# Reordering the head of a fused windowed-attention and swish-gated MLP kernel: v on another queue, weights in two loads, scores ahead of v products

## The chip, the cores and the metric

The kernel runs on one core of a Trainium2 chip. The metric is device time in microseconds (us). The core has five engines that run their own instruction streams in order: PE (TensorE, matrix products and transposes), ACT (ScalarE, exp, tanh and copies), DVE (VectorE, elementwise work), POOL (GpSimd, masks, casts, and loads that change the type) and SP (SyncE, loads and stores). SP, ACT and POOL ask for transfers; 16 DMA engines carry them out.

## The reference

```python
# q, k, v: (4, 8, 768, 64) float32; n_sink = 4, window = 128
scores = q @ k.T / 8
keep = (col < 4) | ((row - col >= 0) & (row - col < 128))
a = softmax(where(keep, scores, -1e9))
x = (a @ v) -> (3072, 512)                  # tokens x (heads * 64)
h = x @ w_in                                # (3072, 2048)
g = h / (1 + exp(-beta * h))
out = g @ w_out                             # (3072, 512) float32
```

Each query sees the first four keys (the sinks) and a window of 128.

## The kernel before

**Units.** The tokens are cut into 8 tiles T of 384 rows (two per batch). A unit `n` is one tile of one pair of heads; four units make a tile, 32 units in all. Units 0 to 3 are the first tile, 4 to 7 the second. For one unit: q and k are loaded as float32 by SP (`load_qk`, L520, 192 KB each), cast to bfloat16 (`cast`, L606: q of units 0 to 3 on ACT, all else on POOL), transposed by PE (`transpose_in`, L619) and copied out of PSUM by one DVE or ACT copy (L626). `scores` multiplies in two halves of two PSUM banks each (L665; for units 0 to 3 an additive mask is put there first by PE, L654), and ACT takes the exp (L673) into `E`. `attend` multiplies `E` with v (L736; from units 4 on also the sinks, L725), `normalise` divides (L745, L747), and `transpose_out` (L764, L768) puts the result into `xT`. From unit 12 on, DMA transposes take the place of PE's.

**The MLP.** A tile has 16 blocks of hidden columns. A block is four matmuls, one for each pair of heads `c` (`hidden_matmul`, L780), so that it is complete only when all four units of the tile are in `xT`; then tanh on ACT (L788) and the gate on DVE (L801). The second product (`project`, L809) adds up 16 blocks for each 128 rows. Ahead of tile 0's whole blocks, the matmuls with `c` = 0 to 2 of the first two blocks are issued; only `c` = 3 waits for unit 3.

**Loads.** v of tile 0 comes as three loads on POOL's queue that cast to bfloat16 on the way (`load_v`, L528). w_in comes as four loads on POOL's queue, each of four of the 16 blocks (`load_w_in`, L564, rows of 2 KB in memory), w_out as eight (`load_w_out`, L569). The loads of q and k of units 4 to 7 wait on SP for the landing of the first w_in load.

**What sets the order.** The program is first a graph of steps. `Prog.order` places them by a cost model: at each point the step that can start earliest, and of several the one written first. Each engine then gets a fixed list, with semaphore waits, and executes it strictly in that order. Constants of this model (`QUEUE`, `MIX`, the rates and weights of `transfer`) cost nothing at run time, but they move steps. In stretches where the model expects PE to wait ahead of the first hidden blocks, it puts in filler matmuls (L448), which keep PE's clock up and are no work.

The call that opens the head:

```python
    for n in range(4):
        for x in range(2):
            load_qk(n, x)
    load_v(0, 0, [ADD[0][0]])
    ...
    for n in range(3):
        cast(n)
        if n < 2:
            load_v(0, n + 1, [("k16", n)])
    load_w_in(0, 4, 0, 4, [("q_stage", 2, 0)])
```

Of the kernel before, what the change touches and what calls it, by code (L numbers as in the profile page):

```python
# [18 lines left out]
TT = 384  # L19
# [5 lines left out]
HEAD1 = 32  # L25

# [47 lines left out]
class Node:  # L74
# [3 lines left out]
                 "place", "dma", "mode", "work", "hard")  # L78

    def __init__(self, id, eng):  # L80
        self.id, self.eng = id, eng
        self.items = []
        self.busy = self.lag = 0.0
        self.preds = {}
        self.succs = []
        self.open = 0
        self.ready = self.done = 0.0
        self.place = None
        self.dma = None
        self.mode = 128  # L90
        self.work = 0.0
        self.hard = set()


class Prog:
# [12 lines left out]
    QUEUE = {"sp": (1200.0, 1.0), "act": (1200.0, 1.0), "gp": (2100.0, 3.0)}  # L108
    TAIL, MIX, RING = 900.0, 1.07, 8
# [27 lines left out]
    def op(self, eng, fn, r=(), w=(), x=(), dma=None, busy=100.0, lag=None, after=(), mode=None,  # L137
           seq=None):
# [28 lines left out]
        if dma is not None:  # L167
            self.dma_count[dma] = self.dma_count.get(dma, 0) + 16
            node.dma = (dma, self.dma_count[dma])
            node.work = lag  # L170
# [22 lines left out]
    def landings(self, placed):  # L193
# [9 lines left out]
        while True:  # L203
            now, later = [], []
            for q, ns in queue.items():
                if head[q] < len(ns):
                    at = ns[head[q]].place + self.QUEUE[q][0]
                    (now if at <= t else later).append((at, q))
# [5 lines left out]
            whole = sum(self.QUEUE[q][1] for _, q in now)  # L214
            rate = {q: (self.MIX if len(now) > 1 else 1.0) * self.QUEUE[q][1] / whole for _, q in now}
# [12 lines left out]
    def round(self, took, freed):  # L228
# [10 lines left out]
        def best(e):  # L239
            q = left[e]  # L240
            while head[e] < len(q) and q[head[e]].place is not None:
                head[e] += 1
            if head[e] == len(q):
                return None
            last = q[min(head[e] + self.AHEAD[e], len(q) - 1)].id
            c = [n for n in can[e] if n.id <= last]
            if not c:
                return None
            n = min(c, key=lambda n: (max(n.ready, free[e]), n.id))
            at = max(n.ready, free[e])  # L250
            if n.dma is not None and issued[e] >= self.RING and freed:
                at = max(at, freed[e][issued[e] - self.RING] if issued[e] - self.RING < len(freed[e]) else at)
            return at, n
# [100 lines left out]
def bass_streamingllm_window__then__act_swish_beta_kernel(  # L354
# [42 lines left out]
    stage = {t: [sb(f"{t}_stage{z}", (128, 2, 6, D), F32) for z in range(4)] for t in "qk"}  # L397
    land = [sb(f"land{z}", (128, 2, 2, 3, 2, D), BF16) for z in range(4)]
    qk16 = [sb(f"qk16_{z}", (128, 2, 3, 2, D), BF16) for z in range(NQK)]
    v_aug = sb("v_aug", (128, 4, 2, 6, D + 2), BF16)  # L400
    v_sink = sb("v_sink", (128, NPAIR, 2, D1), BF16)
    k_rows = sb("k_rows", (NPAIR, NSINK, 2, D), BF16)
    k_sink = sb("k_sink", (128, NPAIR, 128), BF16)
    qkT = [sb(f"qkT{z}", (128, 2, 2, TT), BF16) for z in range(4)]
    E = [sb(f"E{z}", (128, 2, 768), BF16) for z in range(2)]
    E_sink = [sb(f"E_sink{z}", (128, TT), BF16) for z in range(2)]
# [25 lines left out]
    def transfer(size, rate, busy=470.0):  # L432
        return {"busy": busy, "lag": size / rate}
# [8 lines left out]
    def constants():  # L442
        fill("dve", ones32[:, :], 1.0, ["ones32"])
        op("act", lambda e: e.activation(scratch[:, :], ones32[:, 0:1], AF.Exp, bias=0.0, scale=1.0),
           r=["ones32"], w=["scratch"], busy=1500.0)
        fill("dve", ones[:, :], 1.0, ["ones"])
        fill("dve", zeros[:, :], 0.0, ["zeros"], busy=350.0)
        P.filler = (lambda e: e.matmul(acc[1][:, 0:128], ones[:, :], ones[:, :], start=True, stop=True),  # L448
# [66 lines left out]
    def load_qk(n, x, after=(), queue="sp"):  # L515
# [5 lines left out]
           dma=f"{name}{pb}_{half}", seq="loads " + queue, **transfer(2 * TT * D * 4, 335))  # L521

    def load_v(T, c, after=()):
# [6 lines left out]
           dma=f"vb{kb}", **transfer(H * 128 * D * 4, 256, 900.0))  # L530

    def land_qk(n, x, after=()):

        b, hp, half, pb = place(n)
        for hh in range(2):
# [3 lines left out]
               dma=f"l{pb}{half}{x}{hh}", **transfer(TT * D * 4, 256, 780.0))  # L539

    def land_v(n, after=()):
        b, hp, _, pb = place(n)
        half = place(n)[2]
        for hh in range(2):
# [3 lines left out]
               w=[("v", pb, 3 * half + c, hh) for c in range(3)], after=after, dma=f"lv{pb}{half}{hh}", **transfer(TT * D * 4, 256, 780.0))  # L548
# [13 lines left out]
    def load_w_in(c, cs, m, ms, after=()):  # L562
        here = slice(m * 128, (m + ms) * 128)
        op("gp", lambda e: e.dma_start(w_in16[:, c:c + cs, here], w_in_src[:, c:c + cs, here]), after=after,  # L564
           w=[("w_in", cc, mm) for cc in range(c, c + cs) for mm in range(m, m + ms)],
           dma=f"wi{c}_{m}", **transfer(cs * ms * 128 * 128 * 4, 345, 740.0))

    def load_w_out(m, ms, after=()):
        op("gp", lambda e: e.dma_start(w_out16[:, m:m + ms, :], w_out_src[:, m:m + ms, :]), after=after,  # L569
           w=[("w_out", mm) for mm in range(m, m + ms)],  # L570
           dma=f"wo{m}", **transfer(ms * 128 * NOUT * 4, 345, 740.0))

    def load_sinks(after=()):
        s = k[:, :, 0:NSINK, :].rearrange("b (g h) s d -> (b g) h (s d)", h=2)
        for hh in range(2):
            op("gp", lambda e, hh=hh: e.dma_start(k_rows[:, :, hh, :].rearrange("n s d -> n s d"),
               k[:, :, 0:NSINK, :].rearrange("b (g h) s d -> h (b g) s d", h=2)[hh]),
               w=[("k_rows", hh)], after=after, dma=f"sk{hh}", busy=650.0, lag=300.0)
            rows = slice(HEAD1 * hh, HEAD1 * hh + NSINK)
            sv = v[:, :, 0:NSINK, :].rearrange("b (g h) s d -> s h (b g) d", h=2)[:, hh]  # L580
            op("gp", lambda e, rows=rows, hh=hh, sv=sv: e.dma_start(v_sink[rows, :, hh, 0:D], sv),
               w=[("v_sink", hh)], r=["v_sink"], after=after, dma=f"sv{hh}", busy=650.0, lag=400.0)
# [17 lines left out]
    def cast(n):  # L600
# [3 lines left out]
        for x, name in enumerate("qk"):  # L604
            eng = "act" if n < 4 and x == 0 else "gp"
# [3 lines left out]
               **(act(TT) if eng == "act" else {"busy": 460.0, "lag": 100.0}))  # L609
# [18 lines left out]

    def keys_of(pb, rows, kb):
        return qkT[pb][rows, kb // 3, 1, kb % 3 * 128:kb % 3 * 128 + 128]  # L630
# [4 lines left out]
    def scores_sink(n):  # L635
        pb = place(n)[3]
        op("pe", lambda e: e.matmul(s_ps[:, 0, 0:TT], k_sink[:, n // 8 * 4 + n % 4, :],  # L637
                                    queries_of(pb, slice(0, 128), 3, 3), start=True, stop=True),
           r=["k_sink", ("k_sink", 0), ("k_sink", 1), ("qkT", pb, 1)], w=["s0"], **pe(TT))
        op("act", lambda e: e.activation(E_sink[n % 2][:, :], s_ps[:, 0, 0:TT], AF.Exp, bias=0.0,  # L640
# [3 lines left out]
    def keys_read(pb, half, runs):  # L644
        return [("qkT", pb, x) for x in sorted({half, *(kb // 3 for kb, _, _ in runs)})]

    def scores(n, c, banks, names):

        _, _, half, pb = place(n)
# [22 lines left out]
        src = (s_ps if names[0] == "s0" else h_ps)[:, 0:2, 0:TT]  # L672
        op("act", lambda e: e.activation(both, src, AF.Exp, bias=0.0, scale=SCALE),  # L673
# [37 lines left out]
    def attend(n):  # L711
# [9 lines left out]
        with P.together("pe"):  # L721
            for mm in range(3):
                m, at = 3 * half + mm, mm * 2 * D1
                if half == 1:
# [4 lines left out]
                       r=[("E_sink", z), "v_sink", ("v_sink", 0), ("v_sink", 1)], w=["av"],  # L729
                       **pe(130))  # L730
                for hh in range(2):
                    kbs = range(m + 1) if half == 0 else (m - 1, m)
                    for x, kb in enumerate(kbs):
# [6 lines left out]
                           w=["av"], **pe(65))  # L740

    def normalise(n):
# [3 lines left out]
           x=["av"], w=[("rden", z)], **dve(225.0))  # L746
# [3 lines left out]
           r=[("rden", z)], x=["av"], w=[("o_norm", o)], **dve(475.0))  # L750
# [56 lines left out]
    def project(T, t, m, bank, name, eng="act", cols=slice(0, NOUT), queue="sp"):  # L807
# [4 lines left out]
        if m == NM - 1:  # L812
# [7 lines left out]
            else:  # L820
# [5 lines left out]
               r=[("out_sb", z)], dma=f"o{z}", **transfer(128 * width * 4, 389))  # L826
# [7 lines left out]
    op("act", lambda e: e.dma_start(beta_stage[:, :], moe_beta.rearrange("(m p) -> m p", p=128)),  # L834
       w=["beta_stage"], dma="beta", busy=500.0, lag=100.0)
    for n in range(3):
        cast(n)
        if n < 2:
            load_v(0, n + 1, [("k16", n)])
    load_w_in(0, 4, 0, 4, [("q_stage", 2, 0)])  # L840

    select(ident32[:, :], ones32[:, :], [[1, 32]], ALU.is_equal, 0.0, 0, -1, ["ones32"], ["ident32"])
    transpose_in(0)
    for n in range(4):
        if n < 3:
            transpose_in(n + 1)
        if n == 0:
            cast(3)
            load_w_in(0, 4, 4, 4, [("q_stage", 3, 0)])
            for m in (8, 12):  # L850
                load_w_in(0, 4, m, 4, [("k_stage", 3, 0)])
            for y in range(4, 8):
                for x in range(2):
                    load_qk(y, x, [("w_in", 0, 0)])
            for c in range(3):
                load_v(1, c, [("w_in", 0, 4)])
            fill("gp", k_sink[:, :, :], 0.0, ["k_sink"], busy=1800.0, after=[("k_stage", 3, 0)])
            load_sinks([("k_stage", 3, 0)])
            masks([("k_stage", 3, 0)])
        scores(n, 0, (s_ps[:, 0, :], s_ps[:, 1, :]), ("s0", "s1"))  # L860
        scores(n, 1, (h_ps[:, 0, :], h_ps[:, 1, :]), ("h0", "h1"))
        if n > 0:
            transpose_out(n - 1, acc[0], "acc0", "dve")
        attend(n)
        normalise(n)
    op("pe", lambda e: nc.tensor.transpose(acc[0][:, 0:16], beta_stage[:, :], ident32[0:16, 0:16]),
       r=["beta_stage", "ident32"], w=["acc0"], **pe(64))
    op("dve", lambda e: e.tensor_scalar(beta_half[:, :], acc[0][:, 0:16], 0.5, None, ALU.mult),
       x=["acc0"], w=["beta"], **dve(100.0))
    for i in range(2):  # L870
# [4 lines left out]
    transpose_out(3, acc[0], "acc0", "act")  # L875
# [12 lines left out]
    for s in range(-2, S_END + NM):  # L888
        i = block_of(s) if 0 <= s < S_END else None
        if i is not None:  # L890
            hidden(i, 3 if i < 2 else 0)
        later = []
        for n, step in AGENDA.get(s, ()):
# [8 lines left out]
            if step in ("a", "b") and n < XBAR:  # L902
                c = "ab".index(step)
                if n < 8 and c == 1:
                    scores(n, c, (h_ps[:, 0, :], h_ps[:, 1, :]), ("h0", "h1"))
                else:
                    scores(n, c, (s_ps[:, 0, :], s_ps[:, 1, :]), ("s0", "s1"))
# [10 lines left out]
        if s == 0:  # L918
            for m in range(0, 8, 2):
                load_w_out(m, 2, [("q_stage", 0, 1)])  # L920
        if s == 2:
            for m in range(8, NM, 2):
                load_w_out(m, 2, [("q_stage", 1, 1)])
# [67 lines left out]
```

## Time and profile before

| what | value |
|---|---|
| median of 3 runs | 229.73 us (229.33 to 229.84) |
| profiled execution, its own time | 229.27 us |
| its span, first to last instruction | 227.5 us |
| granted TensorE clock | 1.0 |
| DMA: packets, bytes, mean rate | 96853, 28.53 MB, 125 GB/s |
| HBM read, written | 27.34 MB, 6.29 MB |
| first complete hidden block of tile 0 closes | from 20.48 us |
| first hidden block of tile 1 | 47.11 us |

All durations below are of the profiled execution; it lies 0.46 us under the median of the runs, and its span 1.77 us under its own time. In the profile's lines, PE is a matmul and PEld the load of its weights, L12 is a line of the kernel, "x4" a count of instructions, and `<-` stands between what is written and what is read. The queues are named q0 (POOL's, which can cast), q1 (SP's) and q10 (ACT's).

### The profile page before, as it was taken

To read this page: it belongs to the slowest core of one execution; us is meant where nothing else is said; L and a number is where in the kernel's file an instruction comes from. 1 tells how busy PE (TensorE), PEld (TensorE's weight loads), DVE (VectorE), ACT (ScalarE), POOL (GpSimd) and SP (SyncE) were. 2 spreads that over 40 slices of the span, in tenths; PEclk is the share of its full clock that TensorE was granted. 3 is DMA by queue.
4 is the path that set the end of the run, shared out by engine and by line. 5 is a ranking of instruction groups with operands and counts; after the bars stand their busy time and mean duration, and the time that the engine had idled before them with its cause. 6 is when DMAs were issued, how large, how long until landed. Compare 5 with 4: busy or idle time off the path is not lost.

```text
span 227.5 us, 4449 instructions
## 1 busy us (share of the span) xinstructions
PE 219.9 (97%) x1759; PEld 121.7 (53%) x1759; DVE 132.2 (58%) x261; ACT 141.9 (62%) x223; POOL 128.6 (57%) x190
## 2 busy tenths in 40 slices
PE   7798989999999999999999999999999999999995
PEld 5355555545555555555555555555555555555544
DVE  5455887569977666566555555665656555443300
ACT  3655886477787666657767666656675764545411
POOL 7788996799975969494939679594600000000000
PEclk9999999999999999999999999999999999999999
DMA  6999999999997999999999989899932202111022
GB/s 163 204 193 220 246 192 208 244 208 176 122 98 117 104 131 151 119 125 128 140 102 142 115 122 162 118 101 147 140 41 63 64 19 63 49 46 46 9 86 92
DMA packets 96853, 28.53 MB, mean 125 GB/s; under 512 B 83376, under 2 KB 93888, under 8 KB 96832
## 3 DMA queue, kind: packets, MB, share of 16 engines
q0 software_dynamic: 62352, 11.32, 65.5%
q1 hardware_dynamic: 34304, 16.79, 33.8%
q8 instruction: 14, 0.23, 0.4%
q10 hardware_dynamic: 176, 0.14, 0.2%
q14 instruction: 7, 0.06, 0.1%
HBM read 27.34 MB, written 6.29 MB: 148 GB/s over the span
## 4 chain that ended last, share of the span: by engine, by line
PE 87%; DMA 7%; ACT 2%; POOL 1%; SPq 1%; issue 1%; DVE 0%; ACTq 0%
PE acc L809 34%; PE h_ps L780 33%; DMA v_aug<-in_v_dram 6%; PE s_ps L736 5%; PE s_ps L693 4%; PE acc L780 2%; PE h_ps L809 2%; DMA k_stage<-in_k_dram 2%; PE s_ps L725 1%; PE s_ps L637 1%; PE s_ps L665 1%; SPq L520 1%; PE s_ps L619 1%; POOL land L538 1%; PE h_ps L665 1%; POOL qk L606 1%
## 5 line engine op out<-in xcount | busy, mean ns | idle before, releaser
L788 ACT ACTIVATE th<-h_ps,beta_half 128x384 f32<-128x384 f32 x120 | 69.5, 581 | 55.6 <-PE h_ps L780 55.1
L809 PE MATMUL acc<-w_out,g 128*128 128x512 bf16 x368 | 101.5, 380 | 0.0
L780 PE MATMUL h_ps<-xT,w_in 128*128 128x384 bf16 x480 | 96.8, 326 | 0.0
L801 DVE SCALAR_TENSOR_TENSOR g<-th,h_ps 128x384 bf16<-128x384 f32 x120 | 65.6, 549 | 45.7 <-ACT th L788 45.0
L780 PEld LDWEIGHTS h_ps<-xT,w_in 128*128 128x128 bf16 x480 | 46.4, 98 | 40.4 <-DVE g L801 0.5
L809 PEld LDWEIGHTS acc<-w_out,g 128*128 128x128 bf16 x368 | 32.8, 98 | 28.0 <-issue 4.0
L538 POOL DMA_DIRECT2D land<-in_q_dram x40 | 30.9, 773 | 28.5 <-DVE rden L745 28.5
L547 POOL DMA_DIRECT2D v_aug<-in_v_dram x40 | 30.9, 773 | 0.0
L538 POOL DMA_DIRECT2D land<-in_k_dram x40 | 30.9, 773 | 0.0
L701 ACT ACTIVATE E<-s_ps 128x1536 bf16<-128x1536 f32 x20 | 28.8, 1442 | 0.3 <-PE s_ps L693 0.3
L707 DVE TENSOR_TENSOR E<-E,mask 128x1536 bf16<-128x1536 bf16 x20 | 19.2, 958 | 16.1 <-ACT E L701 16.1
L817 ACT ACTIVATE out_sb<-acc 128x512 f32<-128x512 f32 x23 | 13.7, 598 | 10.2 <-PE acc L809 10.0
L736 PE MATMUL s_ps<-v_aug,E 128*128 128x65 bf16 x384 | 19.4, 193 | 0.6 <-DMA v_aug<-in_v_dram 0.6
L736 PEld LDWEIGHTS s_ps<-v_aug,E 128*128 128x128 bf16 x384 | 17.0, 97 | 4.7 <-issue 1.4
L747 DVE TENSOR_TENSOR o_norm<-s_ps,rden 128x384 bf16<-128x384 f32 x32 | 17.7, 555 | 0.9
L673 ACT ACTIVATE E<-s_ps 128x768 bf16<-128x768 f32 x16 | 13.0, 809 | 2.3 <-PE s_ps L665 1.9
L626 DVE COPY qkT<-s_ps 128x768 bf16<-128x768 bf16 x10 | 9.5, 955 | 5.8 <-PE s_ps L619 5.7
L693 PE MATMUL s_ps<-qkT 64*128 64x256 bf16 (+2 forms) x144 | 10.1, 254 | 0.0
L745 DVE RECIPROCAL rden<-s_ps 128x6 f32<-128x6 f32 x32 | 6.1, 192 | 6.6 <-PE s_ps L736 6.3
L680 DVE TENSOR_TENSOR E<-E,mask 128x768 bf16<-128x768 bf16 x16 | 9.1, 581 | 1.5 <-ACT E L673 1.4
L528 POOL DMA_DIRECT2D v_aug<-in_v_dram x9 | 8.2, 915 | 2.3 <-DMA w_in<-in_moe_w_in_dram 1.7
L619 PE MATMUL s_ps<-ident,qk 128*128 128x128 bf16 x72 | 7.4, 227 | 2.1 <-POOL qk L606 0.7
(65 smaller groups left out, 145.4 us busy)
## 6 DMA issues: line engine op xcount, KB each, us to landing
out_dram<-out_sb SPq DMA_DIRECT2D x23, 256.0 KB, 2.6
q_stage<-in_q_dram SPq DMA_DIRECT2D x12, 192.0 KB, 7.1
k_stage<-in_k_dram SPq DMA_DIRECT2D x12, 192.0 KB, 8.0
w_in<-in_moe_w_in_dram POOLq DMA_DIRECT2D x4, 512.0 KB, 8.6
w_out<-in_moe_w_out_dram POOLq DMA_DIRECT2D x8, 256.0 KB, 8.4
land<-in_q_dram POOLq DMA_DIRECT2D x40, 48.0 KB, 3.5
land<-in_k_dram POOLq DMA_DIRECT2D x40, 48.0 KB, 3.8
v_aug<-in_v_dram POOLq DMA_DIRECT2D x40, 48.0 KB, 3.4
```

Source lines behind the costliest of these rows:

```text
L538: op("gp", lambda e, d=d, s=s: e.dma_start(d, s), w=[("land", pb, half, x, hh)], after=after, dma=f"l{pb}{half}{x}{hh}", **transfer(TT * D ...
L547: op("gp", lambda e, d=d, s=s: e.dma_start(d, s), w=[("v", pb, 3 * half + c, hh) for c in range(3)], after=after, dma=f"lv{pb}{half}{hh}", ...
L693: op("pe", lambda e, at=at, w=w, kb=kb, qb=qb, nq=nq, hh=hh, rows=rows, bank=bank: e.matmul(s_ps[:, 2 * hh + bank, at:at + w], keys_of(pb, ...
L701: op("act", lambda e: e.activation(E[z][:, :, :], src, AF.Exp, bias=0.0, scale=SCALE), x=list(S_NAMES), w=[("E", z, 0), ("E", z, 1)], **ac ...
L707: op("dve", lambda e: e.tensor_tensor(E[z][:, :, :], E[z][:, :, :], m.unsqueeze(1).to_broadcast([128, 2, 768]), ALU.mult), r=[("E", z, 0), ...
L736: last=(x == len(kbs) - 1): e.matmul(av_ps[:, at + hh * D1:at + hh * D1 + D1], E[z][:, hh, col:col + 128], v_aug[:, pb, hh, kb, 0:D1], sta ...
L747: op("dve", lambda e: e.tensor_tensor(o_norm[o][:, :, :, :].rearrange("p m h d -> p (m h) d"), src[:, :, 0:D], rden[z][:, :].unsqueeze(2). ...
L780: op("pe", lambda e: e.matmul(bank, w_in16[:, c, m * 128:(m + 1) * 128], xT[:, c, T * TT:(T + 1) * TT], start=(c == 0), stop=(c == 3)), r= ...
L788: op("act", lambda e: e.activation(th[i % 3][:, :], bank, AF.Tanh, bias=0.0, scale=beta_half[:, m:m + 1]), x=[name], r=["beta"], w=[("th", ...
L801: op("dve", lambda e: e.scalar_tensor_tensor(g[T % 2][:, m, :], th[i % 3][:, :], 1.0, bank, ALU.add, ALU.mult), r=[("th", i % 3)], x=[name ...
L809: op("pe", lambda e: e.matmul(bank[:, 0:width], g[T % 2][:, m, t * 128:(t + 1) * 128], w_out16[:, m, cols], start=(m == 0), stop=(m == NM ...
L817: op("act", lambda e: e.activation(out_sb[z][:, 0:width], bank[:, 0:width], AF.Copy, bias=0.0, scale=0.5), x=[name], w=[("out_sb", z)], ** ...
```

## The change

- v of units 0 to 3 is loaded by six uncast float32 loads of 128 KB on ACT's queue (`load_v32`), into a new tile `v_stage`, and cast to bfloat16 by POOL (`cast_v`), one step for each unit. `beta` is asked for first; ACT's dummy exp, which brings in the function table, now stands behind these loads.
- w_in comes in two loads of eight blocks each, with rows of 4 KB in memory. The first is placed behind the v cast of unit 0, the second behind that of unit 2.
- For units 0 to 3, `transpose_first` takes the place of `transpose_in`: q and k go to two PSUM banks and are copied out by ACT (q) and DVE (k) separately. q of these units is cast by DVE, not ACT.
- In the written order, the scores of unit `n + 1` stand ahead of the v products of unit `n`. The v products of units 0 to 3 go to `acc[1]`; unit 3's scores use the banks of `tr` and `av`. The outputs of units 0 to 3 are transposed after all four.
- Three blocks, not two, have their first three matmuls issued ahead.
- Of w_out, the first piece is asked for ahead of v of units 4 to 7. The sink tiles have 36 rows, not 128.
- The cost model has a weight for each transfer, and other rates.

```diff
+    def load_v32(x, c):
+        src = v[0, 4 * x:4 * x + 4, c * 128:c * 128 + 128, :].rearrange("h p d -> p h d")
+        op("act", lambda e: e.dma_start(v_stage[:, c, 4 * x:4 * x + 4, :], src), w=[("v_stage", x, c)],
+           dma=f"v{x}{c}", seq="loads act", **transfer(4 * 128 * D * 4, 240, 520.0, 0.45))
+    def cast_v(n):
+        op("gp", lambda e: e.tensor_copy(v_aug[:, n, :, 0:3, 0:D].rearrange("p h c d -> p c h d"),
+                                         v_stage[:, :, 2 * n:2 * n + 2, :]),
+           r=[("v_stage", n // 2, c) for c in range(3)],
+           w=[("v", n, kb, hh) for kb in range(3) for hh in range(2)], busy=460.0, lag=100.0)
...
-            eng = "act" if n < 4 and x == 0 else "gp"
+            eng = "dve" if n < 4 and x == 0 else "gp"
...
+    def transpose_first(n):
+        z = n % NQK
+        for which, name in enumerate("qk"):
+            bank, at = ((tr_ps, "tr"), (av_ps, "av"))[which]
...
+            eng = "act" if which == 0 else "dve"
+            op(eng, lambda e, eng=eng, dst=dst, src=src: (e.copy if eng == "act" else e.tensor_copy)(dst, src),
+               x=[at], w=[("qkT", n, 0) if which else ("qT", n)], **(act(TT) if eng == "act" else dve(480.0)))
...
-    load_v(0, 0, [ADD[0][0]])
+    op("act", lambda e: e.dma_start(beta_stage[:, :], moe_beta.rearrange("(m p) -> m p", p=128)),
+       w=["beta_stage"], dma="beta", busy=500.0, lag=100.0)
     for n in range(4):
         for x in range(2):
             load_qk(n, x)
...
+    for c in range(6):
+        load_v32(c // 3, c % 3)
+    op("act", lambda e: e.activation(scratch[:, :], ones32[:, 0:1], AF.Exp, bias=0.0, scale=1.0),
+       r=["ones32"], w=["scratch"], busy=1500.0)
+    cast(0)
+    cast(1)
+    cast_v(0)
+    load_w_in(0, 8, [("v", 0, 0, 0)])
+    cast(2)
+    cast_v(1)
+    load_sinks(1, [("v", 1, 0, 0)])
...
+    transpose_first(1)
+    first_scores(0)
+    cast(3)
+    cast_v(2)
+    load_w_in(8, 8, [("v", 2, 0, 0)])
+    cast_v(3)
+    for n in range(4):
+        if n < 2:
+            transpose_first(n + 2)
+        if n < 3:
+            first_scores(n + 1)
+        if n == 2:
+            for y in range(4, 8):
+                for x in range(2):
+                    load_qk(y, x, [("w_in", 0, 0)])
...
+            load_w_out(0, 2, [("v", 3, 0, 0)])
+            for c in range(3):
+                load_v(1, c, [("v", 3, 0, 0)])
+        attend(n, acc[1], "acc1")
+        normalise(n, acc[1], "acc1")
+    for n in range(4):
+        transpose_out(n, *((av_ps, "av") if n % 2 else (tr_ps, "tr")), "dve" if n < 2 else "act")
-    for i in range(2):
+    for i in range(3):
         with P.together("pe"):
             for c in range(3):
                 hidden_matmul(i, c)
```

In the changed kernel's lists, POOL executes: the casts of k of units 0 and 1, `cast_v` of unit 0, the first w_in load, `cast_v` of unit 1, the cast of k of unit 2, two small loads of sink keys, the cast of k of unit 3, `cast_v` of unit 2, the second w_in load. On PE, the transposes of q of unit 4 stand ahead of hidden block 8, and those of k of unit 4 ahead of block 10; before, both stood behind block 13.

More of the change, by code (lines that the diff above doesn't have):

```diff
@@ L90, in __init__ @@
         self.mode = 128
-        self.work = 0.0
+        self.work, self.weight, self.late = 0.0, 1.0, 0.0
         self.hard = set()
@@ L213, in landings @@
                 continue
-            whole = sum(self.QUEUE[q][1] for _, q in now)
-            rate = {q: (self.MIX if len(now) > 1 else 1.0) * self.QUEUE[q][1] / whole for _, q in now}
+            weight = {q: queue[q][head[q]].weight for _, q in now}
+            mix = self.MIX if len(now) > 1 and max(weight.values()) > self.HEAVY else 1.0
+            rate = {q: mix * w / sum(weight.values()) for q, w in weight.items()}
             step = min(left[queue[q][head[q]].id] / rate[q] for _, q in now)
@@ L248, in best @@
                 return None
[L249 to L253, printed above, removed]
+            out = issued[e] - self.RING
+            room = freed[e][out] if freed and 0 <= out < len(freed[e]) else 0.0
+            at = {n.id: max(n.ready, free[e], room if n.dma is not None else 0.0) for n in c}
+            n = min(c, key=lambda n: (at[n.id], n.id))
+            return at[n.id], n
         while any(n.place is None for n in self.nodes):
@@ L520, in load_qk @@
         op(queue, lambda e: e.dma_start(d, s), w=[(name + "_stage", pb, half)], after=after,
-           dma=f"{name}{pb}_{half}", seq="loads " + queue, **transfer(2 * TT * D * 4, 335))
+           dma=f"{name}{pb}_{half}", seq="loads " + queue, **transfer(2 * TT * D * 4, 290 if n not in (1, 2) or x else 170, 520.0))
+    def load_v32(x, c):
[7 more added lines that the diff above has]
+           w=[("v", n, kb, hh) for kb in range(3) for hh in range(2)], busy=460.0, lag=100.0)
     def load_v(T, c, after=()):
@@ L547, in land_v @@
             op("gp", lambda e, d=d, s=s: e.dma_start(d, s),
-               w=[("v", pb, 3 * half + c, hh) for c in range(3)], after=after, dma=f"lv{pb}{half}{hh}", **transfer(TT * D * 4, 256, 780.0))
+               w=[("v", pb, 3 * half + c, hh) for c in range(3)], after=after, dma=f"lv{pb}{half}{hh}", **transfer(TT * D * 4, 256, 780.0, 0.4))
     def turn(n):
@@ L644, in keys_read, with scores @@
     def keys_read(pb, half, runs):
-        return [("qkT", pb, x) for x in sorted({half, *(kb // 3 for kb, _, _ in runs)})]
-    def scores(n, c, banks, names):
+        return [("qT", pb), *(("qkT", pb, x) for x in sorted({half, *(kb // 3 for kb, _, _ in runs)}))]
+    def scores(n, c, names):
+        src = h_ps if names[0] == "h0" else s_ps[:, 0:2, :] if names[0] == "s0" else s_ps[:, 2:4, :]
+        banks = [src[:, hh, :] for hh in range(2)]
         _, _, half, pb = place(n)
@@ L832, in bass_streamingllm_window__then__act_swish_beta_kernel, with first_scores @@
             load_qk(n, x)
[L833 to L851 removed]
+    for c in range(6):
[9 more added lines that the diff above has]
+    load_sinks(1, [("v", 1, 0, 0)])
+    select(ident32[:, :], ones32[:, :], [[1, 32]], ALU.is_equal, 0.0, 0, -1, ["ones32"], ["ident32"])
+    transpose_first(0)
+    op("pe", lambda e: nc.tensor.transpose(acc[1][:, 0:16], beta_stage[:, :], ident32[0:16, 0:16]),
+       r=["beta_stage", "ident32"], w=["acc1"], **pe(64))
+    op("dve", lambda e: e.tensor_scalar(beta_half[:, :], acc[1][:, 0:16], 0.5, None, ALU.mult),
+       x=["acc1"], w=["beta"], **dve(100.0))
+    def first_scores(n):
+        pairs = [("s0", "s1"), ("h0", "h1")] if n < 3 else [("tr", "av"), ("s0", "s1")]
+        for c in range(2):
+            scores(n, c, pairs[c])
+    transpose_first(1)
[5 more added lines that the diff above has]
+    for n in range(4):
+        if n < 2:
+            transpose_first(n + 2)
+        if n < 3:
+            first_scores(n + 1)
+        if n == 2:
             for y in range(4, 8):
@@ L854, in bass_streamingllm_window__then__act_swish_beta_kernel @@
                     load_qk(y, x, [("w_in", 0, 0)])
+            fill("gp", k_sink[:, :, :], 0.0, ["k_sink"], busy=550.0, after=[("v", 3, 0, 0)])
+            masks([("v", 3, 0, 0)])
+            load_sinks(0, [("v", 3, 0, 0)])
+            load_w_out(0, 2, [("v", 3, 0, 0)])
             for c in range(3):
[L856 to L869, printed above, removed]
-    for i in range(2):
+                load_v(1, c, [("v", 3, 0, 0)])
[4 more added lines that the diff above has]
+    for i in range(3):
         with P.together("pe"):
@@ L918, in bass_streamingllm_window__then__act_swish_beta_kernel @@
         if s == 0:
-            for m in range(0, 8, 2):
-                load_w_out(m, 2, [("q_stage", 0, 1)])
+            for m in range(2, 8, 2):
+                load_w_out(m, 2, [("w_in", 0, 0)])
         if s == 2:
             for m in range(8, NM, 2):
-                load_w_out(m, 2, [("q_stage", 1, 1)])
+                load_w_out(m, 2, [("w_in", 0, 8)])
             for n in range(8, 12):
```

97 lines of the change are left out of this document (52 added, 45 removed).

## The prediction

> **What bounds the kernel now.** I read the page first, then the busy time by stretches, the chain that ended last, and the DMA landings one issue at a time. The page's first part:
>
> ```profile
> PE 219.9 (97%) x1759; PEld 121.7 (53%) x1759; DVE 132.2 (58%) x261; ACT 141.9 (62%) x223; POOL 128.6 (57%) x190
> ```
>
> Share of the span: TensorE (PE) looks full, so the question is where it is not, and where it is busy with filler. By stretches (start:end, length, then busy time of each engine, clock, DMA share, GB/s):
>
> ```profile
> 12.40:20.50 8.10, 7.51 (x98) 4.77 (x99) 4.93 (x13) 3.61 (x5) 6.38 (x8) 1.00 1.20 200
> 20.50:31.10 10.60, 10.60 (x75) 6.30 (x75) 8.40 (x16) 9.03 (x18) 10.21 (x26) 1.00 1.49 226
> 31.10:33.30 2.20, 1.54 (x19) 0.69 (x18) 1.49 (x3) 2.20 (x5) 2.20 (x4) 1.00 1.24 205
> 33.30:47.00 13.70, 13.45 (x141) 7.09 (x142) 8.84 (x21) 8.33 (x13) 10.04 (x15) 1.00 1.30 227
> 47.00:214.00 167.00, 166.91 (x1290) 91.08 (x1288) 102.10 (x195) 109.64 (x171) 90.36 (x119) 1.00 0.99 105
> ```
>
> From 47 to 214 PE is idle 0.09 us, and the change removes no real PE work, so this kernel can only win or lose ahead of 47 us: in the head, and in the 0.66 us hole at 31 to 33. The chain (start, length, what) in the head:
>
> ```profile
> 6.96 5.41 DMA v_aug<-in_v_dram
> ...
> 12.41 0.30 PE s_ps L736 x4
> ...
> 18.66 0.59 PE acc L780 x3
> 19.25 0.49 PE h_ps L780 x3
> ...
> 19.95 0.49 ACT xT L768
> ...
> 20.48 0.34 PE acc L780
> ...
> 24.28 1.30 PE acc L780 x8
> ```
>
> PE waits for the last v (landing 12.4), works the attention of units 0 to 3, and runs whole hidden blocks (4 matmuls, 0.65 us) from 20.48, with 1.08 us of them done before. Block 8 starts at 24.28+0.65 = 24.93. Landings (last column: us from issue; the issues stand at 8.26, 10.17 and 14.90), and the packets that flowed from 15.0 to 18.5 and from 19 to 22:
>
> ```profile
> w_in<-in_moe_w_in_dram POOLq DMA_DIRECT2D x1, 512.0 KB, 6.6
> ...
> w_in<-in_moe_w_in_dram POOLq DMA_DIRECT2D x1, 512.0 KB, 7.5
> ...
> q_stage<-in_q_dram SPq DMA_DIRECT2D x1, 192.0 KB, 6.6
> ...
> q0 software_dynamic: 693, 0.69, 122.1%
> ...
> q0 software_dynamic: 391, 0.39, 77.6%
> q1 hardware_dynamic: 397, 0.29, 39.7%
> ```
>
> The first w_in piece lands at 14.85, the second at 17.7. q of unit 4, issued by SP at 14.90 behind that first landing, moves no packet until 18.5, while POOL's queue streams weights; then the queues alternate packet for packet. It lands at 21.5. PE needs it only at 28.95, so this delay is hidden now.
>
> **The change, part by part.** All sums are on the profiled execution: span 227.5, time 229.27 (1.77 around it). The median of runs is 229.73, 0.46 above; I shift by that at the end. 0.2% (0.46 us) is about what a measurement of this kernel can tell.
>
> *v on ACT's queue.* Six 128 KB loads asked from 1.3 us on, instead of three cast loads asked at 2.91, 4.98, 6.96 and landed at 10.2, 11.5, 12.4. The first half of v is 1536 rows of 256 bytes, as many packets as the first six q and k loads have (256 rows of 768 bytes each); if the two queues alternate packet for packet, they end together, and the sixth load, k of unit 2, landed at 3.69+5.2 = 8.9. Bounds: 6.1 (the fourth load's landing, if small rows pass faster) to 10.85 (halfway between the landings 10.2 and 11.5, no gain from the queue). I take 8.8, by the row of 8.9 and a little under it, since nothing else is asked for ahead of v on its queue but beta. ACT's issues cost 0.44+6x0.47 = 3.3 us, so its table load (1.28) and dummy exp (0.20), done at 2.77 now, end at about 5.7. An SP issue was once held 1.82 us; three such would free ACT at 9.9. ACT's work for units 0 to 3 is 8 exps at 0.71 to 0.81 and 4 half copies at 0.48, 8.0 us, so 13.8 to 17.9. Neither is last, see below.
>
> *Casts.* DVE casts q0 to q3: not in the trace; between the 0.35 of DVE's 128x384 copy (L768) and POOL's 0.50; off the path, as q lands before k. POOL now waits for v behind k1's cast; queued behind it are w_in, k2 and k3. v lands 8.8, cast 0.50, gap 0.3 (as 6.67 to 6.96): **w_in is issued at 9.6, not 8.26.** Then POOL: issue 0.75, v cast 0.50, k2 0.50, two k_rows issues 1.05, k3 0.50, gaps: k3 is ready at 13.1 instead of 11.43.
>
> *Two w_in DMAs of 1024 KB.* First bytes after 2.1 (the 8 KB beta load's landing), then 5.4: the two pieces before took 5.3 from the last v (12.4) to 17.7, and 2x2.85 = 5.7 by their spacing. I give the 4 KB rows no speed, because no row shows them. First half: 9.6+2.1+5.4 = **17.1**, for blocks 0 to 7. The second is queued right behind, lands about 22.7 and is not last.
>
> *Unit 3's chain.* From k3 13.1: transposes 0.35, copy 0.5, scores 0.6, two exps 1.5, v products 0.55, reciprocal and multiply 0.8, transposes 0.35, copy 0.5, semaphores 0.5: 18.75. Nine opening matmuls of blocks 0 to 2 (1.47) run meanwhile from 17.1, so PE closes block 0 at 18.8, and with 0.49+5x0.65 and the sink transposes (0.18) is ready for block 8 at 22.7.
>
> *What is late next.* In the changed order PE's transposes of q of unit 4 stand ahead of block 8. SP still asks for it when the first w_in DMA lands: 17.1+6.6 = 23.7, cast and semaphores 0.6, transposes 0.17: **block 8 at 24.5.** PE stands 1.6 us. So the gain of the head hangs on w_in plus 7.4, not on attention, which has that much slack. From there 8 blocks 5.2 and the rest of units 4 and 5 (0.50): 30.2, where before was at 31.1. **0.9 gained.**
>
> *The hole at 31 to 33.* Before, products with w_out can't fill it: the first piece, issued 26.41, landed 6.7 later at 33.1. Now that piece is asked for ahead of v of units 4 to 7, and four products (0.86) stand in the hole. I take back 0.66. Bounds: 1.0 if the products also shorten what follows; 0 if k of unit 7 is late. It landed at 29.6, 14.7 after the batch was opened at 14.90; opened at 17.1 it lands by 31.8, or near 30.8 if it shares less with the first weights, and with a 0.55 cast PE wants it landed by 31.1. v of units 4 to 7 (30.4 at the latest now) moves behind one w_out piece, some 1.3 us by the pieces' spacing, and is wanted about 33.8 (34.74 less the 0.9 gained): covered.
>
> *Later.* The same bytes flow, and PE does the same work. The smaller memsets (k_sink was 1.83 on POOL, off the path) and 36-row sinks save nothing on PE. Reordered steps from 47 on cost nothing while v (53.2) and q and k of units 8 to 11 keep ahead; the change puts unit 8's v products six blocks later, which covers them.
>
> Sum: 0.9+0.66 = 1.6. 229.27-1.6 = 227.7 profiled, **228.1** on the runs.
>
> **A rule against it.** POOL's cast at 43.77 took 0.85 instead of 0.50 beside DVE's two-input mask multiply. The Trainium skill (SBUF — State Buffer, on the shared port pair and the "DVE blocks DMA" trap) says that DVE's fp32 SBUF copies also lock GpSimd out, its descriptor writing included; before has no such copy on DVE, so no run yet shows it for casts.
>
> **Rivals.**
> - *q of unit 4 is not late* (0.18): if its packets alternate at once, as at 19 to 22, the 1.6 us stand goes: 226.5. For: 4 KB rows put fewer packets ahead of it. Against: 15 to 18.5 above, no SP packet in 3.5 us.
> - *DVE's casts hold POOL up* (0.10): three of them lie ahead of the w_in issue, 0.35 each as at 43.77: w_in 1.05 later, gain 0.5: 229.2. Against: POOL's casts in the head wait for landings, with room between.
> - *Slower: v comes no sooner* (0.14). All queues share the same engines; if q, k and v together end at 12.4 as now, half of v is there at 10.85, w_in is asked for at 11.65, lands 19.15, block 8 starts 26.55: 1.15 lost, 0.66 regained: 230.2. It turns slower when the first half of v lands after 10.4. For: 0 to 5 us is the only time with free DMA. Against: before's v was asked for late, its last at 6.96. The Trainium skill (DMA: Bandwidth & Descriptors, "Issuing engines are not separate DMA queues") sides with this rival: several issuers save only issue time. The packet counts agree on sharing.
> - *No net change* (0.06): the hole is not filled and v lands at 9.7: 229.7. It is also the case in which the change does not do what it says, the new queue only swapping the order of q, k and v.
>
> **The numbers.** Forecast 0.52, with its own range 227.3 to 229.2: 0.5 each way on when w_in lands (5.3 to 5.7 for its bytes, and 0.3 on v), and most of the hole's bounds. The rivals as given. Faster: 0.52+0.18+0.09 = 0.79; same 0.07; slower 0.14. Range 226.5 to 230.2, from the first rival to the third.
>
> **What would show it.** Right: POOL's first w_in issue near 9.6 and landing near 17; PE idle ahead of block 8 behind POOL's cast of q_stage; L843 products before 33 us; nothing new after 47. Wrong: v landing after 10; ACT's table load after 8 with PE waiting for exp; w_in's second half ending a wait; idle PE after 47 from a reordered step.

## The result and the profile after: 240.65 us, 4.9% slower

| | before | after |
|---|---|---|
| median of the runs | 229.53 us (228.75 to 229.84) | 240.65 us (240.21 to 241.37) |
| ratio | | 1.0493, 95% interval 1.0455 to 1.0531 |
| span of the profiled execution | 227.5 us | 239.0 us |

The forecast was 228.1 us with a range of 226.5 to 230.2. It missed on the wrong side, by far more than any rival had allowed for.

The page's first part and two of the stretches, of the changed kernel:

```profile
PE 231.1 (97%) x1743; PEld 124.8 (52%) x1770; DVE 133.1 (56%) x264; ACT 141.3 (59%) x224; POOL 122.4 (51%) x189
```

```profile
31.10:33.30 2.20, 2.04 (x22) 1.06 (x22) 2.09 (x4) 1.73 (x4) 1.75 (x3) 1.00 1.44 200
47.00:214.00 167.00, 165.12 (x1222) 86.85 (x1246) 99.32 (x189) 104.74 (x162) 88.48 (x120) 1.00 1.00 102
```

TensorE (PE) counts 11.2 us more busy time with no more work, at a granted clock of 1.00. Between 47 and 214 us it gets through 1246 weight loads where it got through 1288 before (of the matmuls, 1222 against 1290, a few records are missing after), and stands only 1.9 us. So most of the loss is neither in the head nor in a visible wait: the same steps take longer on PE.

The chain that ended last shows which. In it a step's length runs to the start of the next step. One unit with sinks, as it stood before (start, length, what):

```profile
114.72 0.44 PE s_ps L693 x8
115.15 0.75 PE acc L809 x3
...
116.56 0.65 PE acc L809 x3
...
117.86 0.16 PE s_ps L637
118.02 0.06 PE s_ps L725
118.07 0.12 PE s_ps L736 x4
```

The sink scores (L637) take 0.16, then three times 0.06 for a sink product (L725) and 0.12 for four v products (L736): 0.70 us for the unit. A unit of the same tile after:

```profile
130.60 0.27 PE s_ps L670
130.87 0.16 PE s_ps L759
131.03 0.23 PE s_ps L770 x4
...
132.04 0.05 issue
132.09 0.59 PE acc L843 x2
```

Now 0.27, then three times 0.16 and 0.23: 1.44 us. The 0.05 of issue belongs to the next step, of which one matmul record is missing (x2 for x3, and 0.05 + 0.59 is about the 0.65 of before). Every step of the unit is 0.10 to 0.11 longer, the four v products too, in which nothing was changed. A unit passes seven times between a matmul with 36 rows or columns and one of another shape: into the scores, from the scores (36 columns) to the first product (36 rows), out of it, and in and out for each of the other two. Half of the 32 units have sinks: 16 x (1.44 - 0.70) = 11.8 us, against 11.5 in the span.

By groups one sees nearly nothing. The weight loads of the sink products, before and after (busy us, mean ns | idle ahead of them):

```profile
L725 PEld LDWEIGHTS s_ps<-v_sink,E_sink 128*128 128x128 bf16 x48 | 4.7, 98 | 1.4 <-issue 0.2
```

```profile
L759 PEld LDWEIGHTS s_ps<-v_sink,E_sink 36*128 36x128 bf16 x48 | 4.4, 93 | 6.4 <-issue 3.5 <-ACT out_sb L851 0.7 <-ACT th L822 0.4
```

The load itself is even shorter (93 ns for 98). What grew is the idle column, from 1.4 to 6.4, most of it put down to "issue", a wait that the profile can't name. The timeline shows where it lies. The first sink product of each of these two units, its weight load (PEld) and its matmul, before and after:

```profile
117.69 0.10 PEld L725 LDWEIGHTS s_ps<-v_sink,E_sink 128*128 128x128 bf16 x1
117.85 0.22 PE L725 MATMUL s_ps<-v_sink,E_sink 128*128 128x130 bf16 x1
```

```profile
130.80 0.09 PEld L759 LDWEIGHTS s_ps<-v_sink,E_sink 36*128 36x128 bf16 x1 [0.17 <-issue]
130.80 0.23 PE L759 MATMUL s_ps<-v_sink,E_sink 36*128 36x130 bf16 x1
```

Before, the weights are loaded 0.16 ahead of their matmul, while the sink scores still run (117.69 to 118.02). After, the load starts only with its own matmul. A load takes 0.09 to 0.10, about what each step has grown by; that the lost lead is the whole price is inferred from these sizes, not shown apart.

In the head, three things stood otherwise than forecast. The first w_in load, and PE ahead of block 4:

```profile
w_in<-in_moe_w_in_dram POOLq DMA_DIRECT2D x2, 1024.0 KB, 9.7
```

```profile
20.93 0.21 ACT k_sink L611
21.15 0.21 ACT k_sink L611
...
21.37 0.59 ACT th L822
...
22.60 0.82 PE acc L814 x4
```

The 9.7 is the median of the two loads; the first was issued at 9.01 and took 9.0 us, to 18.0. ACT copies the sink keys (twice 0.21) ahead of the first tanh, so the gate that frees a bank for block 4 ends only at 22.55, and PE, done with blocks 0 to 3, stands 0.5 us. Block 8 starts at 25.54.

### The profile page after: what moved, and what is told of

Read it like the earlier page. It is cut to its first block, busy times and chain, and to the rows that moved or that the text cites. A ratio compares the mean times of both kernels' runs of the same rounds, so it can differ in the third digit from the quotient of the medians.

```text
span 239.0 us, 4451 instructions
## 1 busy us (share of the span) xinstructions
PE 231.1 (97%) x1743; PEld 124.8 (52%) x1770; DVE 133.1 (56%) x264; ACT 141.3 (59%) x224; POOL 122.4 (51%) x189
## 4 chain that ended last, share of the span: by engine, by line
PE 93%; DMA 2%; ACT 1%; issue 1%; DVE 1%; POOL 0%; SPq 0%; ACTq 0%
PE acc L843 33%; PE h_ps L814 33%; PE s_ps L770 7%; PE s_ps L727 3%; PE s_ps L759 3%; PE s_ps L700 2%; PE acc L814 2%; PE s_ps L670 2%; DMA k_stage<-in_k_dram 2%; PE h_ps L843 1%; PE s_ps L798 1%; PE acc L450 1%; PE s_ps L634 1%; PE s_ps L652 1%; PE acc L770 1%
## 5 line engine op out<-in xcount | busy, mean ns | idle before, releaser
L814 PE MATMUL h_ps<-xT,w_in 128*128 128x384 bf16 x480 | 95.4, 326 | 0.3 <-DVE g L835 0.2
L843 PE MATMUL acc<-w_out,g 128*128 128x512 bf16 x341 | 93.6, 380 | 1.5 <-issue 0.6
L814 PEld LDWEIGHTS h_ps<-xT,w_in 128*128 128x128 bf16 x480 | 45.3, 98 | 39.2 <-DVE g L835 1.6
L561 POOL DMA_DIRECT2D v_aug<-in_v_dram x40 | 30.2, 756 | 0.0
L770 PE MATMUL s_ps<-v_aug,E 128*128 128x65 bf16 x336 | 20.8, 195 | 0.1
L770 PEld LDWEIGHTS s_ps<-v_aug,E 128*128 128x128 bf16 x336 | 14.3, 98 | 5.5 <-issue 1.4
L781 DVE TENSOR_TENSOR o_norm<-s_ps,rden 128x384 bf16<-128x384 f32 x28 | 15.5, 555 | 0.9
L759 PE MATMUL s_ps<-v_sink,E_sink 36*128 36x130 bf16 x48 | 10.9, 227 | 0.0
L673 ACT ACTIVATE E_sink<-s_ps 36x384 bf16<-36x384 f32 x16 | 7.6, 477 | 2.5 <-PE s_ps L670 2.4
L621 POOL CAST qk<-k_stage 128x384 bf16<-128x384 f32 x12 | 6.5, 542 | 4.2 <-DMA k_stage<-in_k_dram 4.0
```

What stands on the lines that cost most here:

```text
L561: op("gp", lambda e, d=d, s=s: e.dma_start(d, s), w=[("v", pb, 3 * half + c, hh) for c in range(3)], after=after, dma=f"lv{pb}{half}{hh}", ...
L759: op("pe", lambda e, at=at, mm=mm: e.matmul(av_ps[:, at:at + 2 * D1], E_sink[z][:, mm * 128:mm * 128 + 128], v_sink[:, n // 8 * 4 + hp, :, ...
L770: last=(x == len(kbs) - 1): e.matmul(av_ps[:, at + hh * D1:at + hh * D1 + D1], E[z][:, hh, col:col + 128], v_aug[:, pb, hh, kb, 0:D1], sta ...
L781: op("dve", lambda e: e.tensor_tensor(o_norm[o][:, :, :, :].rearrange("p m h d -> p (m h) d"), src[:, :, 0:D], rden[z][:, :].unsqueeze(2). ...
L814: op("pe", lambda e: e.matmul(bank, w_in16[:, c, m * 128:(m + 1) * 128], xT[:, c, T * TT:(T + 1) * TT], start=(c == 0), stop=(c == 3)), r= ...
L843: op("pe", lambda e: e.matmul(bank[:, 0:width], g[T % 2][:, m, t * 128:(t + 1) * 128], w_out16[:, m, cols], start=(m == 0), stop=(m == NM ...
```

## The experiments

**Theory 1** after the two traces: PE pays about 0.1 us whenever it passes between matmuls of 128 rows and columns and smaller ones, and the 36-row sinks make it do so seven times a unit. **Rival:** the loss comes from the steps and loads that the planner put in another order. E1 and E2 take the two parts of the change apart, from either side.

**E1, the change without narrow sinks.**

```diff
-SINKS = HEAD1 + NSINK
+SINKS = 128
```

> The changed kernel with one constant put back: the sink keys, their scores and the sink values get 128 columns or rows again instead of 36; every other part of the change stays. Theory 1 (a sink matmul with 36 rows or columns makes TensorE switch its shape, on the way in and on the way out, and the 16 units with sinks pay 0.76 us each, 12.2 us in all): the loss goes, and what is left of the change shows: 240.65 - 12.2 = 228.5 us, ratio to before 0.992 to 1.000, and one unit with sinks takes 0.71 us from its sink scores to its last v product instead of 1.49. Rival (the loss comes from the steps and loads that the planner put in another order): about 240 us, ratio 1.045 to 1.05, and the unit stays at about 1.5 us.

Measured: 228.59 us, ratio 0.996 (0.9934 to 0.9985). One constant takes the whole loss away and leaves a kernel that is a little faster than both; a unit takes 0.70 us in its chain again. From 1.0493 to 0.996 is 0.0533 of 229.5 us, 12.2 us, the figure of the theory. The rival falls.

**E2, narrow sinks alone.** v_sink, E_sink and k_sink get 36 rows or columns in the kernel before:

```diff
-    v_sink = sb("v_sink", (128, NPAIR, 2, D1), BF16)
+    v_sink = sb("v_sink", (SINKS, NPAIR, 2, D1), BF16)
...
-        op("pe", lambda e: e.matmul(s_ps[:, 0, 0:TT], k_sink[...],
+        op("pe", lambda e: e.matmul(s_ps[0:SINKS, 0, 0:TT], k_sink[...],
```

> The kernel before with the 36-row sink tiles alone: v_sink and E_sink with 36 rows, k_sink with 36 columns, the sink scores written into 36 partitions; order and loads as before. Theory 1 (shape switches): 229.5 + 12.2 = 241.7 us, ratio 1.05. Rival (the loss comes from the new order and queues): 229.5 us, ratio 1.00.

Measured: 241.17 us, ratio 1.0503 (1.0459 to 1.0547). The tiles alone make the loss, in the old order and with the old loads.

**E3, the same number of narrow matmuls with fewer changes of shape.** The three sink products of a unit are issued ahead of its twelve v products:

```diff
-            for mm in range(3):
-                m, at = 3 * half + mm, mm * 2 * D1
-                if half == 1:
+            if half == 1:
+                for mm in range(3):
+                    at = mm * 2 * D1
                     op("pe", ... E_sink ... v_sink ...)
+            for mm in range(3):
+                m, at = 3 * half + mm, mm * 2 * D1
                 for hh in range(2):
```

> The same as the kernel before with 36-row sink tiles, and the three sink products of a unit issued one behind the other ahead of its twelve v products, so that TensorE changes its shape twice for the products instead of six times. Theory 1 (each change costs, some 0.1 us, whatever stands between): 4 of 8 changes go, 0.4 us a unit, 16 units: 241.7 - 6.4 = 235.3 us, ratio 1.025. Rival (each small matmul is slow by itself, wherever it stands): 241.7 us, ratio 1.05.

The matmuls are the same in number and size; in this order part of the sums is lost, most likely of the sinks' share, so only the time is used. Measured: 234.27 us, ratio 1.021 (1.0171 to 1.025). The chain of a unit:

```profile
120.06 0.27 PE s_ps L638
120.33 0.27 PE s_ps L726 x3
120.60 0.48 PE s_ps L739 x12
```

Three sink products behind each other take 0.27, that is 0.16 for the first and 0.055 for each of the others, which is the price they had with 128 rows; of the v products only the first pays. So no narrow matmul is slow by itself, the change of shape is. Three changes are left of seven (the expectation counted eight, the text above seven): 1.02 us a unit, 16 x (1.02 - 0.70) = 5.1 us; by the ratio it is 4.8.

**E4 and E11, where the line lies:** SINKS = 68 and SINKS = 64, otherwise as in E2.

> The kernel before with 68 rows for the sink tiles instead of 128 or 36. Theory 1a (only tiles of up to 64 rows and columns make TensorE switch, as the score matmuls with 64 rows do): 229.5 us, ratio 1.00. Theory 1b (any size other than 128 makes it switch): 241.7 us, ratio 1.05.

> The kernel before with 64 rows for the sink tiles, four fewer than the 68 that cost nothing. Theory 1a (up to 64 rows or columns is another shape of the array, whatever the number): as with 36 rows, 241.2 us, ratio 1.05. Rival (the cost grows as the tile shrinks, or lies at 36 because it is no multiple of 32): between 229.5 and 241 us, or 229.5 us.

Measured: 229.66 us with 68, ratio 1.000 (0.9976 to 1.0024), and 242.01 us with 64, ratio 1.0555 (1.0519 to 1.0591). The chain with 68, and with 64:

```profile
124.54 0.16 PE s_ps L638
124.70 0.06 PE s_ps L726
```

```profile
123.74 0.28 PE s_ps L638
124.02 0.16 PE s_ps L726
```

Four rows make 12 us. 64 costs all that 36 costs, so the price doesn't grow as the tile shrinks; it comes whole between 68 and 64. The Trainium skill (TensorEngine Tiling (Array Packing), "Available Configurations" and "Key Properties") offers a reason: the array can be set up as tiles with 64 or 32 rows or columns, and a change of the tiling mode drains TensorE. It gives no price for the drain. The line between 68 and 64 agrees with it; that these matmuls change the mode, though the kernel asks for no tiling, is inferred, as no trace shows a mode. What the runs show is the price, about 0.1 us.

**E5 and E6, columns and rows.** The kernel before with 36 columns in the sink scores alone, and with 36 rows in the sink products alone.

```diff
-    k_sink = sb("k_sink", (128, NPAIR, 128), BF16)
+    k_sink = sb("k_sink", (128, NPAIR, SINKS), BF16)
```

> The kernel before with 36 columns in k_sink alone: the sink scores are a matmul of 128 rows by 36 columns of weights, while the sink products keep 128 rows (E_sink's other rows are set to zero once). Theory 1 (each change of TensorE's shape costs about 0.11 us, and columns count as much as rows): one change into the scores and one out of them, 2 x 0.11 x 16 units = 3.5 us: 233.0 us, ratio 1.015. Rival (only few rows cost, few columns are free): 229.5 us, ratio 1.00.

```diff
-    v_sink = sb("v_sink", (128, NPAIR, 2, D1), BF16)
+    v_sink = sb("v_sink", (SINKS, NPAIR, 2, D1), BF16)
...
-    E_sink = [sb(f"E_sink{z}", (128, TT), BF16) for z in range(2)]
+    E_sink = [sb(f"E_sink{z}", (SINKS, TT), BF16) for z in range(2)]
```

> The kernel before with 36 rows in v_sink and E_sink alone: the three sink products of a unit have 36 rows, while the sink scores keep 128 columns (the exp reads the first 36). Theory 1 (a change in and a change out for each of the three products, six a unit, about 0.11 us each): 6 x 0.108 x 16 = 10.4 us: 239.9 us, ratio 1.045. Rival (few columns in the scores are what costs): 229.5 us, ratio 1.00.

Measured: 232.28 us, ratio 1.0116 (1.0093 to 1.0139), and 238.71 us, ratio 1.0406 (1.038 to 1.0432): 2.7 and 9.3 us. Together they make 12.0, the whole of E2 (11.5; two and six changes a unit apart, seven together), and few columns cost as few rows do. Both lie under the forecast (3.5 and 10.4), at 0.08 to 0.10 us a change. The chain of one unit with narrow scores alone shows 0.27 for the scores and 0.16 for the first product behind them, the full price of two changes, 0.21 us; so over the 16 units a part of it is hidden, and which part was not followed up.

**E7, the sink-key copies off ACT.** From here on the question is what the rest of the change is worth, so E1 is the base.

```diff
-            op("act", lambda e, hh=hh, rows=rows: e.copy(
+            op("dve", lambda e, hh=hh, rows=rows: e.tensor_copy(
```

> The changed kernel with sinks of 128 rows and with the two copies into k_sink on DVE instead of ACT; TensorE's and POOL's orders stay as they are. Theory A (TensorE's stand near 21 us is ACT's first tanh behind those two copies, 0.43 us, and the chain goes on from there): 228.59 - 0.43 = 228.2 us. Theory B (q of unit 4, cast by POOL at 24.6, ends the next wait whatever comes before it, so the time gained at 21 is waited for at 25): 228.6 us, block 8 at 25.5 us as without the edit.

Measured: 228.53 us, ratio 0.9967 (0.9949 to 0.9984). The interval is 228.4 to 229.2 us at this run's before. It holds Theory B's 228.6 and just misses Theory A's 228.2, but A's figure starts from E1's time, which has an interval of its own of about 0.6 us each way: inconclusive. The trace leans to neither: by the timeline block 8 starts at 25.07 instead of 25.40, TensorE no longer waits for q of unit 4 (0.54 in E1), so B's wait is not what holds the time, and yet the span is the same 226.9 us.

**E9, w_in's first load cut in two**, on top of E7:

```diff
-    load_w_in(0, 8, [("v", 0, 0, 0)])
+    for m in (0, 4):
+        load_w_in(m, 4, [("v", 0, 0, 0)])
```

> As the last kernel, and the first 1024 KB of w_in in two loads of 512 KB. The planner moves more with it: steps on all engines and w_out loads change places. Theory A (the first hidden blocks wait for w_in's first load, and the q and k loads of units 4 to 7 behind its landing: a load of half the size lands some 2.5 us sooner, so that opening products start with unit 2 instead of all together and q of unit 4 is no longer late): block 8 at 24.3 instead of 25.5, 227.4 us. Theory B (the bytes arrive at the same rate, the smaller rows pass some slower, and with q of unit 4 sharing earlier nothing is gained): 228.6 us.

Measured: 231.55 us, ratio 1.0075 (1.0045 to 1.0104), slower than either theory. The first 512 KB landed 5.5 us after its issue instead of 9.1, as expected, and q of unit 4 at 19.3, but the planner put the transposes of unit 5 close behind those of unit 4, with a single hidden block between, and POOL, which issues three v loads and a piece of w_out first, cast q of unit 4 only at 24.7. PE's waits, and three stretches of 2 us from 23 on:

```profile
PE s_ps L634 <- POOL qk L621: 1.3, 1, 1.3
...
PE s_ps L634 <- DVE qkT L641: 1.1, 1, 1.1
```

```profile
23.00:25.00 2.00, 1.00 (x7) 0.39 (x4) 1.53 (x4) 1.54 (x3) 2.00 (x4) 1.00 1.12 311
25.00:27.00 2.00, 1.16 (x10) 0.73 (x10) 0.74 (x2) 0.58 (x1) 2.00 (x5) 1.00 1.23 248
27.00:29.00 2.00, 1.46 (x9) 1.07 (x10) 0.95 (x2) 0.60 (x1) 2.00 (x4) 0.56 1.52 207
```

PE (first busy column) works 1.00 and 1.16 of 2 us, and then the clock column falls to 0.56; matmuls of 326 ns take up to 527. Two of the six runs kept a mean clock of 1.0 and took 230.3 and 230.7 us, the four at 0.993 took 231.4 to 232.1: so the fall of the clock goes with about 1.3 us of the loss, and the rest is there without it. An earlier landing was worth nothing here: POOL's queue and the planned order stood between it and PE, and the stand then cost clock as well. The kernel tells the planned order and the small load apart no further, so Theory A's load by itself is left undecided.

**E10 and E12, the hole at 31 to 33 us.** E10 puts the first w_out piece of E1 back behind the v loads of units 4 to 7; E12 puts it ahead of them in the kernel before, and nothing else.

```diff
-            load_w_out(0, 2, [("v", 3, 0, 0)])
             for c in range(3):
                 load_v(1, c, [("v", 3, 0, 0)])
+            load_w_out(0, 2, [("v", 3, 0, 0)])
```

> The changed kernel with sinks of 128 rows, and the first piece of w_out asked for behind the three v loads of units 4 to 7, as in the kernel before, instead of ahead of them; the planner moves some later steps with it. Theory A (the part of the change that pays is the hole at 31 to 33 us, filled by products that need that piece of w_out): the hole comes back, 0.66 us, 229.2 us, and no product with w_out ahead of 33 us. Theory B (the piece lands in time either way, or other steps fill the hole): 228.6 us.

```diff
+            load_w_out(0, 2, [("w_in", 0, 4)])
             for c in range(3):
                 load_v(1, c, [("w_in", 0, 4)])
```

> The kernel before with one part of the change: the first piece of w_out is asked for ahead of the three v loads of units 4 to 7. The planner moves a few steps around 31 to 50 us with it; v's queue, w_in, the casts and the sinks stay as before. Theory A (apart from the sinks, all that the change gains is the hole at 31 to 33 us, and this piece fills it): 229.5 - 0.66 = 228.9 us, ratio 0.997, products with w_out ahead of 33 us. Rival (the gain that is left without the narrow sinks, 0.9 us, comes from the earlier v and the reordered head): 229.5 us, ratio 1.00.

Measured: E10 230.22 us, ratio 1.0025 (1.0002 to 1.0049); E12 230.03 us, ratio 1.0033 (1.0011 to 1.0055). Taking the piece back costs 1.6 us (1.5 by the ratios), more than twice the forecast: the first product with w_out starts at 34.9 instead of 31.6, and of the 2.0 us that PE stands longer than in E1 from 31.1 to 47, only 0.5 lie ahead of 33.3. Giving the piece alone gains nothing and loses 0.6. In E12 the products with w_out do run early, at 30.0 and at 31.66, yet PE then waits behind them:

```profile
PE s_ps L619 <- DVE qkT L626: 0.4, 1, 0.4
PE s_ps L736 <- DVE E L680: 0.4, 1, 0.4
PE s_ps L637 <- ACT E L673: 0.4, 1, 0.4
```

The chain there runs over ACT and DVE (qkT copy, sink exp, exps, mask); a product that has run earlier is missing later on, where PE waits for this same chain. In E1 the transposes of unit 6 too are done by 31.4, and the waits of PE from 29 to 60 add up to 0.4 us. So in these runs the piece pays only together with the rest of the change. How the 0.9 us of E1 divide between the two stays open; the planner moved some steps in both kernels besides.

## Why the prediction was wrong, point by point

- **"36-row sinks save nothing on PE", and "PE does the same work" from 47 us on** is the step that failed, and with it "this kernel can only win or lose ahead of 47 us". They save nothing, but I had asked only what the smaller tiles could save, and put what they cost at nothing without a reason. The price is in the passage between shapes. E1 and E2 put it at 12.2 and 11.5 us, of a miss of 12.5.
- **The price stood in the trace of before.** The score matmuls have 64 rows (L693), and the product group right behind them takes 0.75 us where the others take 0.65. Seven changes at 0.10, 16 units: 11.2 us, or 239.3 us with all the rest as I forecast it. The kernel's own cost model also has a SWITCH of 95 ns for steps marked with mode 64, and the sink steps carry no such mark, so its planner couldn't see the price either.
- **v on ACT's queue, right and a little better:** POOL had its first half at 8.18 (forecast 8.8), and w_in was issued at 9.01 (9.6). The rival "v comes no sooner" (half of v at 10.85) is out, and with it the time that the Trainium skill's rule (DMA: Bandwidth & Descriptors, "Issuing engines are not separate DMA queues") would have given. The rule itself isn't refuted by that: v was also asked for earlier, from 1.3 us, in smaller loads.
- **w_in's 5.4 us for the bytes was mis-sized:** the load took 9.0 from issue, not 7.5, so it landed at 18.0 instead of 17.1.
- **Block 8 at 24.5 was 1.0 too early** (25.54). q of unit 4 was late as forecast (landed 24.0, forecast 23.7), but PE, which I had ready at 22.7, came only at 25.4 and no longer waited for it; in E1 it waited 0.54, where I had 1.6. The nine opening matmuls stand in PE's list behind unit 3's transposes and began at 19.02, where I let them run from 17.1; and the stand of 0.5 us behind sink-key copies and tanh was not in my sum. Block 15 ended at 31.4 and the transposes of a third unit at 31.6, where before had two units' done by 31.1: the head's 0.9 us are nearly nothing.
- **The hole was filled only in part.** From 31.1 to 47.0 PE was idle 0.91 us before; in E1 it is 0.50, and after 0.81. The chain still runs over ACT's exps and DVE's mask there (32.7 to 34.8 us after, 32.5 to 34.6 in E1). I had let the products fill the hole without asking what ends last behind them (E12).
- **The casts on DVE** held POOL up nowhere that the chain shows: POOL's casts in the head took 0.51 to 0.52 in E1, as before (0.50 to 0.52). The first w_in issue, partly beside a DVE cast, took 0.93 where the second took 0.76, and ended no wait of the chain. A DVE cast took 0.54, a little over my bounds, off the path.
- Without the narrow sinks the change gives 228.59 us (E1), within the forecast's own range of 227.3 to 229.2. That agreement is partly luck: the head gave nearly nothing of its 0.9, and where the 0.9 us of E1 come from stays open.

## What to carry to other kernels

A smaller operand is not free on TensorE: before cutting rows or columns to 64 or fewer, count how often PE passes between that shape and the full one, and price each passage by a group in the trace that already makes one. If a small matmul has to stay, keep it above 64 (68 cost nothing here) or issue the small ones together. And when busy time grows with the same work, look at the chain of one repeated unit, not at the means of the groups.

## What the runs showed of the hardware

- A passage between matmuls of up to 64 rows or columns and full ones costs PE about 0.1 us (0.08 to 0.11 over these runs); 68 rows and columns cost nothing, 64 all of it, and 36 rows after 36 columns is a passage too (0.16 instead of 0.06 for the first product). At such a passage the weights are loaded with their matmul, no longer ahead of it (130.80 for both, against 117.69 and 117.85).
- In the profile this time lies in the steps of the chain and in weight loads that wait for "issue"; the means of the matmuls move by little (the narrow sink scores' from 326 to 338 ns).
- The granted clock fell to 0.56 after only 4 us in which PE was busy a good half of the time (2.16 of 4.0 us, E9), and stood at 0.61 for 2 us more; single stands of 0.5 us left it at 1.00 (E1).
